# RWKV-7 state update and squared-ReLU feed-forward: the triangular inverses computed as half-chunk blocks by row substitution on GpSimd, for all heads and batches at once

## The chip, the cores and the metric

The kernel runs on one core of a Trainium2 chip. The metric is the device time of one execution in microseconds. Each core has TensorE (matrix products, with a separate weight load that overlaps them), VectorE, ScalarE, GpSimd and SyncE (SP, which only issues transfers here), each with its own instruction queue, and 16 DMA engines. In the profile they are called PE and PEld, DVE, ACT, POOL and SP.

## The reference

The input is six arrays r, k, v, w, a, b of 4 batches x 8 heads x 768 steps x 40 channels. Each batch and head carries a 40x40 state through the 768 steps; the result goes through a feed-forward block with 320 inputs, 2048 hidden units and a squared ReLU.

```python
for t in range(S):
    y[:, :, t] = np.einsum('bhd,bhde->bhe', rt, state)
    Sa = np.einsum('bhde,bhe->bhd', state, at)
    state_decay = state * wt[:, :, None, :] - np.einsum('bhd,bhe->bhde', Sa, bt)
    state = state_decay + np.einsum('bhd,bhe->bhde', vt, kt)
# x: y with heads side by side, 3072 tokens x 320
h = np.maximum(x @ w_in, 0.0)
return h * h @ w_out
```

## The kernel before

The sequence is cut into 6 rounds of 128 steps. A chunk is one round of one batch, with its 8 heads; the 24 chunks run in the order round by round, four batches in each (`order`, line 102). Within a chunk the recurrence is turned into products of 128x128 matrices for each head. The coupling between the steps of a chunk is a strictly triangular matrix N for each head, and the chunk needs the inverse of (identity + N), applied to a 128x40 block for each head. Sums of decays are kept as products from the middle of the chunk: `up` and its reciprocal `down`.

The parts of a chunk are Python generators, and a `yield` ends a step:

- `decay` (line 261): transposes of w, b and a by TensorE, cumulative products and two reciprocals by VectorE, then N from `products` (line 206), masked to the upper triangle by VectorE.
- `inverse` (line 220): the inverse by doubling of block sizes in six levels. Each level has, for the two halves of the heads, four transposes (line 235), a copy by ScalarE (line 236), four products and a masked copy (line 244), four products and an addition (line 255), each on 128x512.
- `rest` (line 282): transposes of k, r and v, the masked products A and RV, and the scaling of k and b.
- `chain` (line 314): what depends on the state of the batch: the products with A and the state, the product with the inverse (`heads(xs, g["TT"], ...)`, line 347), the new state, the masked product RX, and the output of the chunk into a `tokens` tile that holds two chunks.
- `ffn` (line 391): for every two chunks, 16 hidden tiles (48 matrix products of 256 columns), ScalarE's ReLU, VectorE's square (line 403), and the products with w_out. A step of it is used as filler, 12 for each chunk (`PER_CHUNK`).

The loop at line 438 interleaves the steps of the chain of chunk i, of `decay`, `inverse` and `rest` of chunk i+1 and of the filler. The weights come in 40 pieces, two beside each step of the inverse; they are stored as 64-bit floats, and `rounded` (line 160) turns each piece into 32-bit floats by nine VectorE instructions after a GpSimd memset (line 164, for the 24 pieces of w_in) and a transfer issued by ScalarE.

The program order is not the order in the queues. The framework plans, at build time, one fixed order for each engine from the program order and its own estimate of when each instruction is ready; on the chip each engine then takes its instructions in that order, and a transfer that must wait holds those behind it in the same queue.

## Time and profile before

| | us |
|---|---|
| median of 3 runs | 1622.65 (1622.06 to 1623.08) |
| profiled execution | 1621.3 |
| span in its profile | 1619.6 |
| TensorE busy | 1550.1 (96%) |
| VectorE busy | 971.6 (60%) |
| ScalarE busy | 315.8 (19%) |
| GpSimd busy | 24.2 (1%) |

In a row of the profile the line of the kernel comes first, then the engine, the operation, what it writes and reads, the shape and the count. Behind the first bar stand the busy time in us of the whole group and the mean duration of one instruction in ns; behind the second, how long the engine was idle just before instructions of the group, and what ended that wait. Overlapping instructions make the busy time smaller than count times mean. TensorE's fp32 products each appear as two instructions, its transposes as one.

### The profile page before, as it was taken

What the parts mean: (1) busy time and instruction counts of PE and PEld (TensorE: products, weight loads), DVE (VectorE), ACT (ScalarE), POOL (GpSimd) and SP (SyncE); (2) the same over time, 40 slices, a digit from 0 to 9 for tenths busy, and PEclk for the clock granted to TensorE, in tenths of its full rate; (3) what the DMA queues carried; (4) which work ended last, traced back from release to release, by engine and by line L of the source; (5) the groups of instructions that cost most, each with busy time, mean ns of one, the idle gap of its engine ahead of it and who ended that gap; (6) DMA issues with size and microseconds to landing.
All of it is one profiled execution on the core that took longest, in us unless ns stands there. A gap on an engine that the chain in (4) does not pass through costs nothing.

```text
span 1619.6 us, 29073 instructions
## 1 busy us (share of the span) xinstructions
PE 1550.1 (96%) x12240; PEld 1399.5 (86%) x12240; DVE 971.6 (60%) x1921; ACT 315.8 (19%) x645; POOL 24.2 (1%) x85
## 2 busy tenths in 40 slices
PE   4866899999999999999999999999999999999999
PEld 3755789899889989989989989989988988988987
DVE  5999986566555645646636636646655565564621
ACT  0111122112112112212212212212211212221211
POOL 3110000000000000000000000000000000000000
PEclk9978799999999999999999999999999999999999
DMA  8223211010100101101101001001010110000000
GB/s 96 64 61 84 67 38 18 18 27 9 22 22 14 27 17 18 27 14 22 26 11 25 13 18 31 13 18 31 9 21 19 18 22 21 15 2 9 2 6 13
DMA packets 162402, 40.87 MB, mean 25 GB/s; under 512 B 152672, under 2 KB 157664, under 8 KB 162272
## 3 DMA queue, kind: packets, MB, share of 16 engines
q1 hardware_dynamic: 156480, 28.52, 10.2%
q10 hardware_dynamic: 5792, 10.49, 2.2%
q8 instruction: 97, 1.59, 0.4%
q14 instruction: 33, 0.27, 0.1%
HBM read 34.08 MB, written 3.93 MB: 23 GB/s over the span
## 4 chain that ended last, share of the span: by engine, by line
PE 87%; DVE 6%; DMA 1%; issue 0%; ACT 0%; DVEq 0%; ACTq 0%
PE ps_w L74 35%; PE ps_f L74 27%; PE ps_c L74 12%; PE ps_w L235 7%; PE ps_w L203 4%; DMA raw<-in_moe_w_out_dram 1%; PE ps_c L353 1%; DVE inv L255 1%; PE ps_w L301 1%; PE ps_c L342 1%; DVE inv_t L227 0%; DVE N L216 0%; DVE signed L175 0%; DVE power L179 0%; DVE inv_g L244 0%; DVE inv_t L228 0%
## 5 line engine op out<-in xcount | busy, mean ns | idle before, releaser
L244 DVE TENSOR_TENSOR inv_g<-ps_w,half 128x512 f32<-128x512 f32 x288 | 197.2, 689 | 207.8 <-PE ps_w L74 205.1
L74 PE MATMUL ps_w<-inv,N 128*128 128x128 f32 x2304 | 287.4, 278 | 0.3 <-DVE RV L216 0.3
L74 PE MATMUL ps_f<-tokens,w_in 128*128 128x256 f32 x1152 | 282.2, 382 | 0.0
L74 PEld LDWEIGHTS ps_w<-inv,N 128*128 128x128 f32 x2304 | 272.7, 193 | 6.6 <-DVE RV L216 0.5
L74 PE MATMUL ps_w<-inv_g,inv_t 128*128 128x128 f32 x1920 | 239.5, 277 | 4.7 <-DVE inv_g L244 4.5
L74 PEld LDWEIGHTS ps_w<-inv_g,inv_t 128*128 128x128 f32 x1920 | 227.7, 192 | 18.0 <-issue 5.6
L255 DVE TENSOR_TENSOR inv<-ps_w,inv 128x512 f32<-128x512 f32 x240 | 165.8, 691 | 116.7 <-PE ps_w L74 115.7
L74 PEld LDWEIGHTS ps_f<-tokens,w_in 128*128 128x128 f32 x1152 | 204.7, 191 | 20.8 <-issue 0.5
L74 PE MATMUL ps_f<-w_out,hid 128*128 128x320 f32 x768 | 220.9, 433 | 0.0
L236 ACT COPY inv_t<-ps_w 128x512 f32<-128x512 f32 x240 | 130.6, 588 | 402.4 <-PE ps_w L235 374.6
L403 DVE TENSOR_TENSOR hid<-hid 128x256 f32<-128x256 f32 x192 | 80.0, 418 | 172.8 <-ACT hid L402 172.8
L74 PEld LDWEIGHTS ps_f<-w_out,hid 128*128 128x128 f32 x768 | 139.6, 190 | 47.6 <-issue 0.2
L402 ACT ACTIVATE hid<-ps_f 128x256 f32<-128x256 f32 x192 | 73.8, 385 | 331.4 <-PE ps_f L74 331.4
L235 PE MATMUL ps_w<-ident,inv 128*128 128x128 f32 x960 | 129.7, 275 | 6.3 <-DVE inv L255 6.0
L235 PEld LDWEIGHTS ps_w<-ident,inv 128*128 128x128 f32 x960 | 109.6, 141 | 26.2 <-DVE inv L255 10.2
L235 PE MATMUL ps_w<-ident,inv_t 128*128 128x128 f32 x192 | 31.9, 294 | 25.3 <-DVE inv_t L228 22.1
L255 DVE TENSOR_TENSOR inv_t<-ps_w,inv_t 128x512 f32<-128x512 f32 x48 | 33.2, 691 | 30.4 <-PE ps_w L74 29.9
L235 PEld LDWEIGHTS ps_w<-ident,inv_t 128*128 128x128 f32 x192 | 23.6, 151 | 29.9 <-issue 24.4
L74 PEld LDWEIGHTS ps_w<-inv_t,inv_g 128*128 128x128 f32 x384 | 46.4, 192 | 3.3 <-issue 0.7
L236 ACT COPY inv<-ps_w 128x512 f32<-128x512 f32 x48 | 28.1, 586 | 105.1 <-PE ps_w L235 85.6
L74 PEld LDWEIGHTS ps_w<-aT,bT 40*128 40x128 f32 x384 | 25.7, 204 | 26.1 <-DVE aT L276 19.1
L74 PE MATMUL ps_w<-aT,bT 40*128 40x128 f32 x384 | 30.6, 304 | 18.2 <-DVE aT L276 18.2
(111 smaller groups left out, 1578.9 us busy)
## 6 DMA issues: line engine op xcount, KB each, us to landing
raw<-in_moe_w_out_dram ACTq DMA_DIRECT2D x16, 320.0 KB
in_w<-in_w_dram SPq DMA_DIRECT2D x24, 160.0 KB
in_a<-in_a_dram SPq DMA_DIRECT2D x24, 160.0 KB
in_k<-in_k_dram SPq DMA_DIRECT2D x24, 160.0 KB
in_b<-in_b_dram SPq DMA_DIRECT2D x24, 160.0 KB
in_r<-in_r_dram SPq DMA_DIRECT2D x24, 160.0 KB
in_v<-in_v_dram SPq DMA_DIRECT2D x24, 160.0 KB
raw<-in_moe_w_in_dram ACTq DMA_DIRECT2D x48, 80.0 KB
```

Of the source, the lines that this page charges most:

```text
L74: nc.tensor.matmul(o, l_, r_, start=start, stop=True, skip_group_check=True)
L203: nc.tensor.transpose(p_[:, q * 128:(q + 1) * 128], pair(x_, q), ident)
L235: nc.tensor.transpose(p_[:, q], src[e][:, q], ident)
L236: nc.scalar.copy(dst[e], p_)
L244: nc.vector.tensor_tensor(gs[e], p_, over4(halves[lv]), Alu.mult)
L255: nc.vector.tensor_tensor(to, p_, to, Alu.add)
L301: nc.tensor.transpose(p_[:, q * 128:(q + 1) * 128], d_[:, q], ident)
L342: nc.tensor.transpose(p_[:, q * 128:(q + 1) * 128], st[:, q].rearrange("p e d -> p (e d)"), ident)
L353: nc.tensor.transpose(p_[:, q * 128:(q + 1) * 128], pair(xn, q), ident)
L402: nc.scalar.activation(h_, p_, Act.Relu)
L403: nc.vector.tensor_tensor(h_, h_, h_, Alu.mult)
```

## The change

N is not masked any more but copied by ScalarE and stored to DRAM for each chunk, as are `up`, `down` and the transposed and scaled a. This part is now called `early`; it runs eight chunks ahead (`LEAD`), and `rest` loads what it needs back from DRAM, one chunk ahead.

The 128x128 inverse is replaced by the inverses of its two diagonal 64x64 blocks, T, and the off-diagonal block of N is applied in the chain: the first 64 rows are solved, multiplied with the off-diagonal block, added, and then the second 64 rows are solved. The chain thus has three products of 64x64 blocks for each head in place of one of 128x128, and four more copies and products that follow one another.

The inverses of a whole round (4 batches x 8 heads x 2 blocks) are computed together by `solve`. The blocks are gathered from DRAM to `half_n`, and the 64 blocks lie on partitions, once for the even and once for the odd columns, 128 in all. Then 63 steps of two instructions each, a product and a subtraction, substitute row by row. The result goes to DRAM, and `rest` loads the part of its chunk. Round 0 is solved on VectorE while chunks 4 to 7 are prepared; round 1 on GpSimd ahead of the loop; round c+2 on GpSimd, requested behind the last chunk of round c.

The square of the hidden tile reads the product in PSUM as one of its factors. Several buffers have fewer copies. The weights are asked for in the first two passes of the loop, 20 pieces in each. The tables `first` and `halves` are gone.

```diff
-    LEVELS = 7
     GB = 2
+    LEAD = 2 * B
...
+    dram = ctx.enter_context(tc.tile_pool(name="dram", bufs=1, space=bass.MemoryType.DRAM))
...
+    def load_early(i):
+        early_loaded[i] = {nm: fetch(ring, src, i) for nm, ring, src in (("w", "w", w), ("b", "ab", b), ("a", "ab", a))}
 
     def load(i):
...
+        loaded[i] = {nm: fetch(nm, src, i) for nm, src in (("k", k), ("r", r), ("v", v), ("b", b))}
...
+    kept_n = [dram.tile([C, H, C], FP32, tag=f"n{i}", name=f"kept_n{i}") for i in range(len(order))]
...
+    kept_t = [dram.tile([B, 2, H, HC, HC], FP32, tag=f"t{c}", name=f"kept_t{c}") for c in range(NCH)]
...
+    def early(i):
...
         nc.vector.reciprocal(down[:, :, MID + 1:C + 1], up[:, :, MID + 1:C + 1])
         nc.vector.reciprocal(up[:, :, :MID], down[:, :, :MID])
+        nc.sync.dma_start(out=kept_up[i][:, :, :C + 1], in_=up[:, :, :C + 1])
+        nc.sync.dma_start(out=kept_down[i][:, :, :C + 1], in_=down[:, :, :C + 1])
...
+        nc.sync.dma_start(out=kept_a[i], in_=aT)
+        yield
+        for e, p_ in enumerate(products(bT, aT)):
+            t_ = turned("N", 2)
+            nc.scalar.copy(t_, p_)
+            nc.sync.dma_start(out=kept_n[i][:, e * NP:(e + 1) * NP, :], in_=t_)
+        yield
...
+    def solve(c, eng):
+        ns = new("half_n", [128, HC, HC], 1)
+        ts = new("half_t", [128, HC // 2, HC], 1)
+        eng.memset(ts, 0.0)
+        flat = ts.rearrange("p j t -> p (j t)")
+        for par in range(2):
+            eng.memset(flat[par * 64:(par + 1) * 64, par::HC + 2], -1.0)
+        at = 0
+        for par in range(2):
+            for bb in range(B):
+                for half in range(2):
+                    rows = slice(half * HC, (half + 1) * HC)
+                    nc.sync.dma_start(out=ns[at:at + H], in_=kept_n[c * B + bb][rows, :, rows].rearrange("s h t -> h s t"))
+                    at += H
+        yield
+        for s in range(HC - 1):
+            n, m_ = s // 2 + 1, HC - 1 - s
+            p_ = new("half_p", [128, 528], 1)[:, :n * m_].rearrange("p (j t) -> p j t", j=n)
+            eng.tensor_tensor(p_, ns[:, s, s + 1:].unsqueeze(1).to_broadcast([128, n, m_]),
+                              ts[:, :n, s:s + 1].to_broadcast([128, n, m_]), Alu.mult)
+            eng.tensor_tensor(ts[:, :n, s + 1:], ts[:, :n, s + 1:], p_, Alu.subtract)
+            yield
+        for par in range(2):
+            dst = kept_t[c].rearrange("b f h (j two) t -> (b f h) two j t", two=2)[:, par]
+            nc.sync.dma_start(out=dst, in_=ts[par * 64:(par + 1) * 64])
+        yield
...
     def rest(i, g):
...
+        nc.sync.dma_start(out=down, in_=kept_down[i][:, :, 1:C + 1])
+        nc.sync.dma_start(out=aT, in_=kept_a[i])
+        nc.sync.dma_start(out=up, in_=kept_up[i][:, :, :C])
+        with nc.allow_non_contiguous_dma(reason="two decays a head and channel"):
+            nc.sync.dma_start(out=ends[:, 0], in_=kept_down[i][:, :, 0])
+            nc.sync.dma_start(out=ends[:, 1], in_=kept_up[i][:, :, C])
...
+        g["T"], g["N"] = new("T", [128, H, HC], 2), new("N21", [HC, H, HC], 2)
+        for half in range(2):
+            nc.sync.dma_start(out=g["T"][half * HC:(half + 1) * HC], in_=kept_t[c][bb, half].rearrange("h j t -> j h t"))
+        nc.sync.dma_start(out=g["N"], in_=kept_n[i][:HC, :, HC:])
+        yield
...
     def chain(i, g):
...
-        xs = by_head(psum(ps_c))
-        heads(xs, g["TT"], lambda h: xr[:, h], True)
-        xn = minus_x.next()
-        nc.scalar.mul(xn[:, :, :D], xs, -1.0)
...
+        xr = new("xr", [128, H, D], 1)
+        nc.scalar.copy(xr[first], x_[first])
+        yield
+        xn = minus_x.next()
+        xs = by_head(psum(ps_c))
+        for h in range(H):
+            mm(xs[first, h], T[first, order_of(h)], xr[first, h], h == 0)
+        nc.scalar.copy(xn[first, :, :D], xs[first])
+        yield
+        for h in range(H):
+            mm(x_[second_, h], N[:, order_of(h)], xn[first, h, :D], False)
+        nc.scalar.copy(xr[second_], x_[second_])
+        yield
+        for h in range(H):
+            mm(xs[second_, h], T[second_, order_of(h)], xr[second_, h], h == 0)
+        nc.scalar.copy(xn[second_, :, :D], xs[second_])
...
-                nc.vector.tensor_tensor(h_, h_, h_, Alu.mult)
+                nc.vector.tensor_tensor(h_, p_, h_, Alu.mult)
...
+    run(several(range(B), prepare))
+    load(0)
+    weave((solve(0, nc.vector), HC + 1), (several(range(B, LEAD), prepare), 4 * B))
+    run(solve(1, nc.gpsimd))
+    run(rest(0, ready[0]))
     for i in range(len(order)):
+        bb, c = order[i]
+        parts = [(chain(i, ready.pop(i)), 10)]
         if i + 1 < len(order):
+            load(i + 1)
+            ready[i + 1] = {}
+            parts.append((rest(i + 1, ready[i + 1]), 6))
+        if i + LEAD < len(order):
+            parts.append((prepare(i + LEAD), 4))
+        if pieces:
+            parts.append((weights(20), 20))
+        parts.append((filler(PER_CHUNK), PER_CHUNK))
+        weave(*parts)
+        if bb == B - 1 and c + 2 < NCH:
+            run(solve(c + 2, nc.gpsimd))
```

`weave` takes its generators' steps in turn, each spread evenly over the longest of them; `several` runs a generator for each of several chunks; `prepare(i)` is the load for chunk i+1 and `early(i)`.

More of the change, by code (lines that the diff above doesn't have):

```diff
@@ L428, in run, with weave @@
             pass
-    load(1)
-    ready = {0: {}}
-    run(decay(0, ready[0]))
-    others = rest(0, ready[0])
-    for _ in inverse(ready[0]):
-        next(others, None)
-        load_weights(1)
-    run(others)
+    def weave(*gens):
+        total = max(n for _, n in gens)
+        for step in range(total):
+            for gen, n in gens:
+                for _ in range((step + 1) * n // total - step * n // total):
+                    next(gen, None)
+        for gen, _ in gens:
+            run(gen)
@@ L457 @@
-        run(this)
-        while left and i + 1 < len(order) and next(second):
-            left -= 1
+            load(i + 1)
[9 more added lines that the diff above has]
+            run(solve(c + 2, nc.gpsimd))
```

211 lines of the change are left out of this document (78 added, 133 removed).

## The prediction

> **What bounds the kernel now.** I read the page's busy lines first, then the slices of the span, then the chain of work that ended last.
>
> ```profile
> PE 1550.1 (96%) x12240; PEld 1399.5 (86%) x12240; DVE 971.6 (60%) x1921; ACT 315.8 (19%) x645; POOL 24.2 (1%) x85
> ...
> PE   4866899999999999999999999999999999999999
> ...
> PEclk9978799999999999999999999999999999999999
> ...
> PE 87%; DVE 6%; DMA 1%; issue 0%; ACT 0%; DVEq 0%; ACTq 0%
> PE ps_w L74 35%; PE ps_f L74 27%; PE ps_c L74 12%; PE ps_w L235 7%; PE ps_w L203 4%; DMA raw<-in_moe_w_out_dram 1%; PE ps_c L353 1%; DVE inv L255 1%; PE ps_w L301 1%; PE ps_c L342 1%; DVE inv_t L227 0%; DVE N L216 0%; DVE signed L175 0%; DVE power L179 0%; DVE inv_g L244 0%; DVE inv_t L228 0%
> ```
>
> TensorE is busy for all but 70 us of the span, and nearly all of that idle time lies in the first five slices. The chain of work says the same by line. Busy time by windows of 100 us (columns: length, PE, PEld, DVE, ACT, POOL with counts, granted clock, DMA share, GB/s) shows two stages with different limits:
>
> ```profile
> 0.00:100.00 100.00, 60.06 (x453) 53.65 (x455) 81.61 (x222) 11.92 (x20) 20.95 (x79) 0.92 0.47 75
> 100.00:200.00 100.00, 77.07 (x609) 68.69 (x606) 94.75 (x255) 14.56 (x28) 3.22 (x6) 0.86 0.28 75
> ...
> 300.00:400.00 100.00, 100.00 (x780) 91.31 (x779) 54.63 (x100) 19.52 (x40) 0.00 (x0) 1.00 0.08 16
> ```
>
> Up to 200 us VectorE sets the pace (94.75 us of the second 100), because it rounds the weights there beside its work for the chunks. After that TensorE has no gap. So in the main stage a change is worth what it takes from or adds to TensorE, until another engine or a queue takes its place.
>
> **What leaves TensorE.** The inverse is gone from it. Its five groups, and the one product of the chain that is replaced:
>
> ```profile
> L74 PE MATMUL ps_w<-inv,N 128*128 128x128 f32 x2304 | 287.4, 278 | 0.3 <-DVE RV L216 0.3
> L74 PE MATMUL ps_w<-inv_g,inv_t 128*128 128x128 f32 x1920 | 239.5, 277 | 4.7 <-DVE inv_g L244 4.5
> L74 PE MATMUL ps_w<-inv_t,inv_g 128*128 128x128 f32 x384 | 47.1, 276 | 0.6 <-DVE inv_g L244 0.6
> L235 PE MATMUL ps_w<-ident,inv 128*128 128x128 f32 x960 | 129.7, 275 | 6.3 <-DVE inv L255 6.0
> L235 PE MATMUL ps_w<-ident,inv_t 128*128 128x128 f32 x192 | 31.9, 294 | 25.3 <-DVE inv_t L228 22.1
> ...
> L74 PE MATMUL ps_c<-xr,inv_t 128*128 128x40 f32 x384 | 45.7, 277 | 0.5 <-DVE inv_t L255 0.5
> L74 PEld LDWEIGHTS ps_c<-RX,in_b 128*64 128x64 f32 x384 | 23.7, 144 | 2.7 <-DVE RX L216 1.5 <-issue 0.8 <-DVE power L173 0.3
> ```
>
> 287.4 + 239.5 + 47.1 + 129.7 + 31.9 = 735.6 us of busy TensorE. The product with the full inverse (16 instructions a chunk, 45.7 us in all, 119 ns each although only 40 columns stream: the 128-column weight load sets it) becomes three products of 64x64 blocks, 48 instructions a chunk. A 64-column weight load takes 23.7 / 384 = 62 ns; I take 65 ns, so 48 x 24 x 0.065 = 75 us. TensorE after: 1550 - 736 - 46 + 75 = 843 us. The feed-forward part, all transposes of inputs and all other products stay.
>
> **What leaves and enters VectorE.**
>
> ```profile
> L244 DVE TENSOR_TENSOR inv_g<-ps_w,half 128x512 f32<-128x512 f32 x288 | 197.2, 689 | 207.8 <-PE ps_w L74 205.1
> L255 DVE TENSOR_TENSOR inv<-ps_w,inv 128x512 f32<-128x512 f32 x240 | 165.8, 691 | 116.7 <-PE ps_w L74 115.7
> ...
> L227 DVE TENSOR_TENSOR inv_t<-N,first 128x512 f32<-128x512 f32 x48 | 30.9, 682 | 0.0
> ...
> L403 DVE TENSOR_TENSOR hid<-hid 128x256 f32<-128x256 f32 x192 | 80.0, 418 | 172.8 <-ACT hid L402 172.8
> L323 DVE TENSOR_TENSOR f<-f,same 128x8 f32<-128x8 f32 x20 | 3.4, 168 | 0.7
> ```
>
> About 490 of its 972 us go (197 + 166 + 31, three groups of the same size as L227, and the mask of N, which becomes a ScalarE copy). Squaring the hidden tile from PSUM instead of SBUF is nothing: L255 reads PSUM and takes 691 ns where L227 without PSUM takes 682. ScalarE gives up the inverse's copies,
>
> ```profile
> L236 ACT COPY inv_t<-ps_w 128x512 f32<-128x512 f32 x240 | 130.6, 588 | 402.4 <-PE ps_w L235 374.6
> ```
>
> and gets 48 copies of N at that 0.59 us and 48 more half-height copies in the chain; it stays under a fifth busy and the copies of N cost nothing, as N is wanted only rounds later. What enters on VectorE is the first round of the substitution. A round is 63 steps of two instructions; step s works on (s//2+1)(63-s) elements a partition, which sums to 22,352, so 44,704 elements and 126 instructions. From the rows of 512 and 256 elements: (682-418)/256 = 1.03 ns an element and about 154 ns an instruction (the 8-element row of 168 ns agrees). 44,704 x 1.03 + 126 x 0.154 = **65 us on VectorE**, once.
>
> **The other five rounds, on GpSimd.** The trace has no two-input operation there. Nearest rows:
>
> ```profile
> L164 POOL MEMSET raw<- 128x512 int32 x24 | 12.7, 533 | 101.6 <-DVE power L179 101.6
> ...
> L135 POOL MEMSET half<- 128x128 f32 x6 | 1.3, 217 | 0.0
> ...
> L121 POOL TENSOR_SCALAR_AFFINE_SELECT upper<-upper 128x128 f32<-128x128 f32 x1 | 0.3, 307 | 0.0
> ```
>
> Memsets give (533-217)/384 = 0.82 ns an element and 112 ns an instruction: the lower bound is 44,704 x 0.82 + 126 x 0.112 = 51 us a round. If two reads and the write go one after another at that rate, 2.47 ns an element, with the select's fixed 200 ns: 110 + 25 = 136 us. I take 115 us, in the upper half, since two operands must be read where the memset reads none. The Trainium skill, GPSIMD Engine Reference, section on elementwise cycle accounting, gives about 2.6 cycles an element at 1.2 GHz for this operation and advises against it there; by that estimate a round is 97 + 25 = 122 us. No run here shows it yet.
>
> Is that hidden? A round serves four chunks. TensorE needs (843 - 75 for the start - 42 for the last feed-forward group) / 22 = 33 us a chunk, 132 us for four. The substitution of round c+2 starts when N of its last chunk is written, in the fourth chunk of round c, and its result is wanted four chunks later; with some 15 us for the store of N, the 16 gathers, the store of T and its load, it needs 130 us. It fits with nothing to spare. If solves ran back to back from 170 us on, with four chunks and the last group (175 us) behind the fifth, the end would be 170 + 5(S+15) + 175 = 420 + 5S: 995 us for S = 115, below what follows. GpSimd decides from S = 143.
>
> **DMA and SyncE.** All new transfers go through SP's queue.
>
> ```profile
> q1 hardware_dynamic: 156480, 28.52, 10.2%
> q10 hardware_dynamic: 5792, 10.49, 2.2%
> ...
> 538.86 0.37 SPq L110 DMA_DIRECT2D in_v<-in_v_dram  x1
> 547.04 0.37 SPq L110 DMA_DIRECT2D in_k<-in_k_dram  x1
> ...
> 548.64 2.78 SPq L385 DMA_DIRECT2D tokens<-tokens  x4
> 551.51 0.52 SPq L110 DMA_DIRECT2D in_r<-in_r_dram  x1
> ```
>
> Small packets cost 0.102 x 16 x 1619.6 / 156480 = 17 ns of an engine, 1.8 KB ones 98 ns. After, a chunk has about 11,800 packets of 256 B and less (b is loaded twice), 2,050 of 512 B and 510 of 2 KB: some 350 engine-us, 22 us over 16 engines. SP goes from 11 issues a chunk to 29.5 (25, and 18 a round); at four in 2.8 us that is 21 us. Both fit into 33 us, at two thirds, so transfers alone add nothing; the issue order is another matter (rival below). The rows also show that this queue isn't in program order: in_v precedes in_k, which the program lists first.
>
> **The start.** Nothing of chunk 0's inverse can be used before the first four chunks are prepared, their N has gone to DRAM and back, and 126 dependent VectorE steps are done. Before, that inverse began after one chunk. The feed-forward part, 503 us of TensorE and the cover for the chain's latencies, cannot start before the weights are rounded and chunks 0 and 1 have ended. Rows for VectorE's list:
>
> ```profile
> L268 DVE TENSOR_TENSOR_SCAN decay<-ps_w,ones 128x64 f32<-128x64 f32 x96 | 25.7, 268 | 4.6 <-PE ps_w L203 4.6
> L271 DVE RECIPROCAL decay<-decay 128x256 f32<-128x256 f32 x24 | 41.4, 1725 | 0.0
> L276 DVE TENSOR_TENSOR aT<-ps_w,decay 128x512 f32<-128x512 f32 x24 | 16.3, 680 | 0.0
> L173 DVE TENSOR_SCALAR power<-power 128x256 int32<-128x256 int32 (+1 forms) x40 | 11.8, 295 | 0.0
> L179 DVE SCALAR_TENSOR_TENSOR power<-raw,signed 128x256 f32<-128x256 uint32 (+1 forms) x40 | 17.7, 443 | 0.0
> ```
>
> Each of these stands for a pair or more of its kind. A chunk's preparation: two groups each, 2 x (25.7 + 41.4 + 16.3) / 24 = 6.9 us; ten of them (eight ahead, two beside chunks 0 and 1), 69 us. Weights: 5 x 11.8 + 4 x 17.7 = 130 us. The solve, 65 us. Three chunks' products and scaling at six 0.68 us instructions each, and two chains, 17 us. Sum 281 us. In the window of 100 to 200 us VectorE ran at 0.95; 281 / 0.95 = 296, and 9 us for first loads: the feed-forward part runs freely from about **305 us**, with about 75 us of TensorE's work done (ten preparations at 3.2, three rests at 5, two chains at 11 us). The cover for all this is only TensorE's remaining early work, which is small, so the start's cost is paid nearly in full: some 230 us of idle TensorE against 70 in the whole run before.
>
> **The sum.** 843 - 75 = 768 us of TensorE remain. In the window of 300 to 400 it was at 1.00, but there the inverse's products filled the gaps between the chain's steps, and the new chain has four more hand-offs between TensorE and ScalarE. Bounds for its share: 1.00, and 0.77 as in the window of 100 to 200. I take 0.93, since the feed-forward part remains as filler and is more than half of the rest: 768 / 0.93 = 826 us. 305 + 826 = 1131 us of span, plus 1621.3 - 1619.6 = 2 us around it; the profiled execution was 1.4 us below the median of 1622.65. **Forecast 1135 us.** Its own range, by shares 1.00 to 0.85 and a start 30 us shorter or longer: 1045 to 1245.
>
> **Rivals.**
>
> *TensorE stays full and the start is shorter.* If the weights' rounding slips into the gaps between the dependent steps of the solve and loading costs less, the start is 260 us with 70 us done and the share 1.00: 260 + 773 + 2 = 1035 us. For it: rounding already interleaved with the inverse in the first windows. Against: VectorE was full there.
>
> *SP is held by the store of T.* The store waits for the last GpSimd step; every load behind it in SP's queue (k, r, v, b, decays, a, w) waits too, and behind those the next chunk's transposes. If the queue's order, fixed at build time, assumes a faster GpSimd than the chip's, a round loses up to S less one chunk of loads already in flight, 115 - 33 = 82 us; half of it, 41 us in five rounds, is 205 us: 1340 us. For it: SP's order is by expected readiness, and the row above shows such an order. Against: a store expected late stands late, and does no harm.
>
> *VectorE and GpSimd hold each other up.* During GpSimd's first round some 230 of the 360 rounding instructions are still open. If each waits for the GpSimd step in progress (0.9 us), 126 of them pass in that round, which adds about 80 us to the start: 1215 us. GpSimd's memsets of the raw weight tiles (L164, which waited 101.6 us for VectorE) stand in the same queue: where one stands among the steps, its wait for VectorE holds the steps behind it. The Trainium skill, SBUF — State Buffer, section Who interferes with whom, states such an exclusive lock for VectorE instructions with two SBUF inputs. Rows before can't show it: GpSimd only wrote.
>
> *Slower: GpSimd becomes the bound.* By 420 + 5S the end passes 1622 us from S = 240 us a round, 1.9 us a step instruction, 4.8 ns an element. At 5.5 ns an element S is 271 us and the time 1775 us. For it: the operands are broadcast along one dimension and strided by 64 elements in the other, and no row has that. Against: it is twice my upper bound.
>
> *The change doesn't do what it says* (rounds not run ahead, one chunk waiting for the next): needs solves in series with the chunks, 305 + 826 + 5 x 115 = 1706 us; the program asks for round c+2 a round early, so this needs a queue that holds everything.
>
> **Chances.** Forecast 0.50, full TensorE 0.10, lock 0.12, SP held 0.18, GpSimd the bound 0.08 (of which 0.02 ends below 1622), in series 0.02. The range 1030 to 1430 leaves out the last two and the tails of the others, some 0.17. A measurement here can tell 0.2% from no change: faster 0.91, within 0.2% 0.01, slower 0.08.
>
> **What would show it.** Right: TensorE near 840 us busy; GpSimd's step instructions of 0.9 us in mean, with idle time between rounds; VectorE full up to some 300 us and half busy after; first feed-forward products after 250 us. Wrong: SP's waits on GpSimd or on the T store of tens of us in each round (SP held); GpSimd without idle time from its first round on (the bound); VectorE rows of the rounding much longer than 295 and 443 ns while GpSimd works (lock); TensorE at 0.99 from 260 us on (full). The forecast fails above all if the start isn't set by VectorE's list or if a GpSimd step costs over 1.2 us.

## The result and the profile after

The changed kernel takes **1538.22 us** (median of 4 runs, 1534.04 to 1542.20) where the kernel before took 1622.87 us beside it (1622.06 to 1625.98): a ratio of 0.9475, 95% interval 0.9445 to 0.9505. It is faster, as predicted, but the forecast was 1135 us and its range ended at 1430 us. The profiled execution spans 1532.3 us, against a forecast span of 1131 us: 401 us are to be explained. Ratios and intervals, here and below, are taken from the faster group of executions where a kernel's executions fell into two groups, so some differ from the ratio of the medians.

The page of the changed kernel: span, busy times, the slices of TensorE, GpSimd and TensorE's granted clock, and the chain that ended last.

```profile
span 1532.3 us, 18790 instructions
...
PE 1062.4 (69%) x7248; PEld 884.2 (58%) x7248; DVE 598.7 (39%) x1330; ACT 202.1 (13%) x453; POOL 566.7 (37%) x702
...
PE   3300025009975989649989769899399994499999
...
POOL 2110000009990079920199700499500899100000
PEclk9555555556897996859967878959799887699999
...
POOL 36%; PE 32%; DMA 11%; DVE 10%; SPq 7%; issue 4%; ACTq 0%; ACT 0%; DVEq 0%; POOLq 0%
```

TensorE has three kinds of loss now. It is almost empty until about slice 9 (340 us). After that it dips at or just behind the end of each of GpSimd's five blocks of work, and its clock, 1.00 from 300 us on in before, dips too. And its busy time is 1062 us where 843 us was forecast. The chain that ended last runs through GpSimd for 36% of the span.

Three stretches of the same execution, cut at TensorE's start and at the last store of T (columns: length, then busy time of PE, PEld, DVE, ACT and POOL with counts, granted clock, DMA share, GB/s):

```profile
0.00:340.00 340.00, 57.76 (x320) 47.64 (x320) 237.65 (x620) 12.63 (x22) 21.08 (x60) 0.57 0.63 106
340.00:1310.00 970.00, 798.05 (x5540) 669.56 (x5540) 313.61 (x617) 150.63 (x340) 545.66 (x642) 0.82 0.51 80
1310.00:1532.00 222.00, 206.59 (x1388) 167.00 (x1388) 47.45 (x93) 38.85 (x91) 0.00 (x0) 0.95 0.20 42
```

GpSimd's steps themselves, by line (count, then busy us and mean ns, then its idle time ahead of them):

```profile
L268 POOL TENSOR_TENSOR half_p<-half_n,half_t 128x462 f32<-128x462 f32 (+46 forms) x315 | 255.6, 811 | 397.3 <-DMA in_k<-in_k_dram 176.1
L270 POOL TENSOR_TENSOR half_t<-half_t,half_p 128x462 f32<-128x462 f32 (+46 forms) x315 | 281.7, 894 | 24.7
```

255.6 + 281.7 = 537 us for five rounds, 107 us a round: the forecast had 115. GpSimd idles 397 us between the rounds. So it isn't slow, it is kept waiting, and what it waits for is shown by SP's waits and, further down, by SP's issues (start, length, issue; x counts issues in a row):

```profile
SPq L274 <- POOL half_t L270: 174.0, 4, 54.5
...
SPq L262 <- POOL half_p L268: 50.7, 1, 50.7
```

The first number is the wait in us, then how often, then the longest. TensorE's longest wait in total:

```profile
PE ps_w L202 <- DMA in_k<-in_k_dram: 150.9, 5, 39.5
```

And SP's issues behind two of the stores of T:

```profile
658.65 2.71 SPq L274 DMA_DIRECT2D kept_t<-half_t  x2
...
670.06 0.53 SPq L113 DMA_DIRECT2D in_k<-in_k_dram  x1
```

```profile
874.59 2.86 SPq L274 DMA_DIRECT2D kept_t<-half_t  x2
...
889.76 0.40 SPq L113 DMA_DIRECT2D in_k<-in_k_dram  x1
...
933.12 31.11 SPq L262 DMA_DIRECT2D half_n<-kept_n  x14
964.33 3.07 SPq L113 DMA_DIRECT2D in_k<-in_k_dram  x1
```

SP stands at the store of T (L274) until GpSimd's last step, 174 us in four waits. The loads of k, r, v, b for the next chunk stand behind it, so TensorE runs dry: it waits 151 us for k, in five waits. When SP goes on, it first catches up on those loads, and only then, from 933 us, comes the burst of 14 of the 16 gathers for the next round: 58 us after the store, 31 us long, 2.2 us a gather, with the loads of the next chunk behind it again. Stores follow one another by 874.59 - 658.65 = 216 us, of which GpSimd works half. Solve and chunks had become a loop through one queue.

### The profile page after: what moved, and what is told of

It reads as the page before. It is cut to its first block, busy times and chain, and to the rows that moved or that the text cites. A ratio compares the mean times of both kernels' runs of the same rounds, so it can differ in the third digit from the quotient of the medians.

```text
span 1532.3 us, 18790 instructions
## 1 busy us (share of the span) xinstructions
PE 1062.4 (69%) x7248; PEld 884.2 (58%) x7248; DVE 598.7 (39%) x1330; ACT 202.1 (13%) x453; POOL 566.7 (37%) x702
## 4 chain that ended last, share of the span: by engine, by line
POOL 36%; PE 32%; DMA 11%; DVE 10%; SPq 7%; issue 4%; ACTq 0%; ACT 0%; DVEq 0%; POOLq 0%
PE ps_f L77 19%; POOL half_t L270 19%; POOL half_p L268 17%; PE ps_c L77 8%; PE ps_w L77 2%; DMA raw<-in_moe_w_in_dram 2%; SPq L262 2%; DMA in_k<-in_k_dram 2%; DMA raw<-in_moe_w_out_dram 2%; DVE half_t L270 2%; DVE half_p L268 2%; PE ps_w L202 2%; SPq L274 1%; SPq L398 1%; DMA kept_down<-down 1%
## 5 line engine op out<-in xcount | busy, mean ns | idle before, releaser
L268 POOL TENSOR_TENSOR half_p<-half_n,half_t 128x462 f32<-128x462 f32 (+46 forms) x315 | 255.6, 811 | 397.3 <-DMA in_k<-in_k_dram 176.1
L270 POOL TENSOR_TENSOR half_t<-half_t,half_p 128x462 f32<-128x462 f32 (+46 forms) x315 | 281.7, 894 | 24.7
L416 DVE TENSOR_TENSOR hid<-ps_f,hid 128x256 f32<-128x256 f32 x192 | 81.2, 423 | 319.2 <-ACT hid L415 319.0
L77 PE MATMUL ps_c<-xr,T 64*64 64x40 f32 x768 | 65.8, 249 | 81.4 <-DMA T<-kept_t 74.5
L77 PEld LDWEIGHTS ps_c<-xr,T 64*64 64x64 f32 x768 | 59.1, 159 | 96.4 <-DMA T<-kept_t 75.0
L202 PE MATMUL ps_w<-ident,in_w 128*128 128x128 f32 x96 | 22.2, 376 | 113.9 <-DMA in_w<-in_w_dram 109.6
L229 DVE TENSOR_TENSOR_SCAN up<-ps_w,ones 128x64 f32<-128x64 f32 x96 | 26.2, 273 | 170.9 <-PE ps_w L202 169.3
L244 ACT COPY N<-ps_w 128x512 f32<-128x512 f32 x48 | 25.8, 589 | 351.0 <-PE ps_w L77 284.0
L218 DVE TENSOR_TENSOR RV<-ps_w,upper 128x512 f32<-128x512 f32 x48 | 30.9, 683 | 64.1 <-PE ps_w L77 64.1
L77 PEld LDWEIGHTS ps_c<-in_v,A 128*128 128x128 f32 x384 | 52.6, 215 | 2.4 <-ACT kvT L297 1.0
```

The source lines that it names most:

```text
L77: nc.tensor.matmul(o, l_, r_, start=start, stop=True, skip_group_check=True)
L202: nc.tensor.transpose(p_[:, q * 128:(q + 1) * 128], pair(x_, q), ident)
L218: nc.vector.tensor_tensor(t_, p_, over4(upper), Alu.mult)
L229: nc.vector.tensor_tensor_scan(up[:, q, MID + 1:C + 1], wT[:, q, MID:], ones, 1.0, Alu.mult, Alu.mult)
L244: nc.scalar.copy(t_, p_)
L268: eng.tensor_tensor(p_, ns[:, s, s + 1:].unsqueeze(1).to_broadcast([128, n, m_]), ts[:, :n, s:s + 1].to_broadcast([128, n, m_]), Alu.mult)
```

## The experiments

Line numbers in the experiments' rows are a few higher than in the changed kernel where lines were added. Kernels with all rounds on VectorE scatter by up to 2.3% between executions, so among those only larger differences, or ranges that don't overlap, are read.

### What the removal alone is worth: no_inverse

```
 before.py, inverse():
-        for lv in range(1, LEVELS): ...transposes, products, masks...
+        for _ in range(3 * (LEVELS - 1)):
+            yield
```

> The kernel before with the six levels of the inverse left out (identity plus the masked N stands for the inverse, so the states and the output are other numbers); all else stays, the full 128x128 product of the chain too. Theory A, as the prediction's first step has it (group times may be subtracted from TensorE's busy time): 1550 - 736 = 814 us of TensorE busy and a time of 885 to 930 us. Theory B (TensorE's groups overlap each other: they sum to 1723 us where the busy time is 1550, so a group is worth about 0.90 of its sum): (1723 - 736) x 0.90 = 888 us busy and a time of 960 to 1010 us.

Measured: 991.17 us (990.15 to 992.20), ratio 0.6114 (0.6102 to 0.6126).

```profile
PE 916.9 (93%) x6480; PEld 773.1 (78%) x6480; DVE 580.0 (59%) x1345; ACT 157.3 (16%) x357; POOL 24.1 (2%) x85
```

Theory B's time; its busy time of 888 us was 29 us short. TensorE's busy time falls by 1550.1 - 916.9 = 633 us and not by the 736 us to which the removed groups sum. Matmuls overlap their neighbours (277 ns each by the mean, 125 ns apart by busy time and count), and the busy time of a group counts overlap with other groups that the union counts once. The first step of the prediction took group sums out of a union: 103 us too much. The run also shows how far the idea could reach: with no substitution to wait for, and before's own order, the kernel ends at 991 us, 144 us under the forecast.

### What GpSimd's rounds cost: one_step

```
-        for s in range(HC - 1):
+        for s in range(HC - 1 if c == 0 else 1):
```

> Rounds 1 to 5 do one of the 63 substitution steps on GpSimd; 62 are left out, so T of these rounds is not the inverse. Theory A (a round is a loop of gathers, solve, store of T, and the loads of about 1.5 chunks that stand behind the store in SP's queue): SP no longer waits for GpSimd, a round takes as long as TensorE needs for four chunks, 135 to 150 us in place of 217, and the whole takes about 1105 us (1060 to 1150). Rival B (all of GpSimd's 120 us a round simply add to the rest): 1532 - 5 x 118 = 940 us.

Measured: 1368.81 us, ratio 0.8438 (0.8421 to 0.8454). Stretches of one_step, as above, cut by eye at 350 us:

```profile
0.00:350.00 350.00, 62.74 (x366) 52.74 (x367) 237.82 (x620) 13.48 (x24) 21.68 (x62) 0.56 0.64 106
350.00:1367.00 1017.00, 972.20 (x6885) 813.01 (x6883) 335.54 (x710) 188.34 (x429) 10.88 (x20) 0.92 0.53 84
```

Both theories missed. With GpSimd all but free (32.6 us of work) the kernel is 169 us faster, no more. The other 236 us of the error (1367.4 - 1131) are a start of 350 us and 972 us of TensorE work behind it, in which TensorE is 96% busy. This run splits the question in three: rounds, start, TensorE's work.

### Where GpSimd's rounds lose it: the queue

*store_late* pins the store of T of rounds 1 to 5 two chunks before the next round starts, so that SP meets it late:

```
+        if bb == B - 2 and c + 1 in stores:
+            stores.pop(c + 1)()      # the store, tc.keep_in_program_order(...)
```

> The changed kernel with the store of T of rounds 1 to 5 issued late: its place in SP's order is pinned two chunks before the first chunk that needs it, instead of wherever the planner expects GpSimd to be done. Theory A (SP, held by that store with the loads of about 1.5 chunks behind it, is what puts the rounds in series): SP's wait at the store falls from 174 us to under 40, the rounds' period from 217 us to some 160-180, and the time to 1400-1460 us. Theory B (the rounds are in series for another reason: one tile for N and gathers that queue behind loads): period and time stay, 1510-1540 us.

Measured: 1463.32 us, ratio 0.9026 (0.9009 to 0.9042). SP's waits for GpSimd in store_late:

```profile
SPq L264 <- POOL half_p L270: 119.6, 3, 50.6
...
SPq L277 <- POOL half_t L272: 64.0, 2, 47.1
```

75 us better than the changed kernel, just short of A's 1460 us: SP still stands still for 184 us, now mostly at the gathers (L264), which wait until the one tile for N is free. *late_and_behind* pins those gathers too, and moves round 1's gathers behind the loads of T of chunks 0 and 1 (the request for round 1's whole solve moves behind the loop's first pass for that):

```
+                    elif c > 1:
+                        tc.keep_in_program_order(nc.sync.dma_start(out=ns[at:at + H], ...))
```

> The store of T pinned late as in the run that did this alone (1463 us), round 1's gathers behind the loads of T as above, and the gathers of rounds 2 to 5 pinned at the end of the round that asks for them, so that SP waits for GpSimd as little as the order allows. Theory A (what is left of SP's waits for GpSimd, 120 us at the gathers and 64 at the stores, holds the loads): 1390-1430 us. Theory B (GpSimd's 125 us and the transfers around it fill a round, wherever the waits stand): 1450-1480 us.

Measured: 1458.29 us, ratio 0.8983 (0.8948 to 0.9017), Theory B's number. Its longest wait of SP for GpSimd is again the store, 231 us in five rounds. Neither place tried in SP's order suits both sides, so the next runs take both kinds of transfer off that queue. *all_gpsimd_queue* sent gathers, store and also the loads of T over GpSimd's queue:

```
-  nc.sync.dma_start(...half_n / kept_t / T...)
+  nc.gpsimd.dma_start(...half_n / kept_t / T...)
```

> All transfers that depend on the substitution (the gathers of N, the store of T and the loads of T) are issued from GpSimd's queue, so that nothing in SP's queue waits for GpSimd. All 63 steps stay. Theory A: SP's waits on GpSimd (174 us at the stores) go, loads for the next chunks run during the solve, a round takes solve 120 + gathers and transfers 30 = about 150 us, and with the start some 60 us shorter the whole takes about 1280 us (1200 to 1350). Rival B (GpSimd's time is on the path whatever the queue): 1480 to 1540 us.

Measured: 1517.24 us, ratio 0.9351 (0.9335 to 0.9367), Theory B's number. The wait only changed hands: the loads of T now wait on GpSimd's in-order queue for TensorE to free the tile T (219 us), and the steps behind them wait too. *solve_queue_gpsimd* leaves the loads of T on SP and moves only gathers and store:

```
-  nc.sync.dma_start(out=ns[...]) ; nc.sync.dma_start(out=dst, in_=ts[...])
+  nc.gpsimd.dma_start(out=ns[...]) ; nc.gpsimd.dma_start(out=dst, in_=ts[...])
```

> The changed kernel with all 16 gathers of a round and the store of T on GpSimd's own queue, where their waits for the solve cost nothing; the loads of T stay on SP. Theory A (SP's hold and the burst of gathers on SP are what made the rounds cost 170 us over the run with one step a round): 1370-1410 us. Theory B (GpSimd's rounds in series set the end, at 125 us of steps, some 15 of gathers and 10 to 20 of store and landing): a period of 150-160 us from 344 us on, the fifth round ending near 1110 us, 222 us behind it, 1340 us by that alone, so TensorE's own work would decide and the time comes out as under A; only a period over 165 us, 1430-1470 us, shows GpSimd as the bound.

Measured: 1461.04 us, ratio 0.9015 (0.9000 to 0.9030). That is in the range in which Theory B sees GpSimd as the bound, but the profile shows something else. SP no longer waits for GpSimd, and from 600 us on TensorE is busy by 95%. The loss has moved to 400 to 600 us; a window of solve_queue_gpsimd, two lines of the weights' rounding in it, and waits of GpSimd and TensorE:

```profile
400.00:500.00 100.00, 26.82 (x67) 14.99 (x65) 91.38 (x110) 3.00 (x8) 84.40 (x81) 0.50 0.14 39
```

```profile
L167 DVE TENSOR_TENSOR signed<-signed,power 128x256 int32<-128x256 int32 (+1 forms) x11 | 11.7, 1068 | 0.3
L164 DVE TENSOR_SCALAR power<-power 128x256 int32<-128x256 int32 (+1 forms) x11 | 10.3, 939 | 0.2
```

```profile
POOL raw L156 <- DVE power L171: 257.6, 13, 102.8
...
PE ps_f L77 <- DVE w_out L172: 83.8, 16, 11.4
```

The same two lines of the rounding in the changed kernel, from 60 to 300 us, where GpSimd has no steps to do:

```profile
L167 DVE TENSOR_TENSOR signed<-signed,power 128x256 int32<-128x256 int32 (+1 forms) x34 | 15.5, 456 | 1.1
...
L164 DVE TENSOR_SCALAR power<-power 128x256 int32<-128x256 int32 (+1 forms) x34 | 10.4, 305 | 0.6
```

With round 0's gathers out early the solve ran ahead of the rounding, and the rounding fell into GpSimd's first round, where the instructions shown take 2.3 to 3.1 times as long, and TensorE waits for the rounded weights (84 us for w_out's). The longest of GpSimd's waits, 102.8 us, is the memset of a raw weight tile (L156): it stands among the steps of the first round, from 307 to 410 us, waits for VectorE's rounding, and holds the steps behind it. These are both halves of the prediction's VectorE and GpSimd rival, in a place where the changed kernel, whose rounding ends before 300 us, does not meet them. *gathers_after0_gpsimd* keeps round 0 on SP, with which the rounding comes first, and moves the later rounds' gathers and stores:

```
-  nc.sync.dma_start(out=ns[...]) ; nc.sync.dma_start(out=dst, in_=ts[...])
+  (nc.sync if c == 0 else nc.gpsimd).dma_start(...)      # both
```

> The changed kernel with the gathers and the store of T of rounds 1 to 5 on GpSimd's own queue; round 0's stay on SP, so that the rounding runs ahead of the solve as in the changed kernel. Theory A (burst on SP, SP's hold, and the rounding slowed beside GpSimd are the three costs, and all three are gone): the rounding is done before 300 us, TensorE is fully loaded from 310-320 us on, 930-970 us of its work behind that: 1290-1350 us. Theory B (GpSimd's rounds set the end even when nothing stands in their way, at 160-170 us from one to the next): 1380-1450 us.

Measured: **1364.86 us** (1360.77 to 1372.13), ratio 0.8421 (0.8388 to 0.8454): between the two theories, 15 us above A's range. It is 0.887 of the changed kernel by the medians, the best that keeps the substitution, and no slower than one_step with its 62 of 63 steps left out. Its stretches, and its gathers on GpSimd's queue:

```profile
0.00:350.00 350.00, 76.92 (x514) 65.96 (x515) 244.55 (x634) 16.04 (x30) 40.78 (x92) 0.62 0.68 110
350.00:1362.00 1012.00, 946.52 (x6735) 790.68 (x6735) 356.49 (x696) 186.93 (x424) 600.80 (x701) 0.91 0.50 84
```

```profile
L262 POOL DMA_DIRECT2D half_n<-kept_n x80 | 64.3, 809 | 228.2 <-DVE half_t L270 169.0 <-DMA kept_n<-N 29.2 <-DMA half_n<-kept_n 28.9
```

GpSimd's five rounds, 107 us of steps each, cost no more here than rounds of one step do in one_step. What the transfers' places in SP's queue made of them was 1538 - 1365 = 173 us. (The edit lets the planner order everything anew, so a part of this may be a better order elsewhere; no run separates the two.)

### The start

*gather0_gpsimd* moves only round 0's gathers to GpSimd's queue:

```
-  nc.sync.dma_start(out=ns[at:at + H], ...)
+  (nc.gpsimd if c == 0 else nc.sync).dma_start(out=ns[at:at + H], ...)
```

> One edit: the 16 gathers of N for round 0 are issued from GpSimd's queue in place of SP's. In the changed kernel they go out between 74 and 183 us, and the profile puts SP's waits before them down to transfers of the raw weights. Theory A (the start is held because gathers on SP share transfer semaphores with the weights' transfers on ScalarE's queue): the gathers are out by about 90 us, the first VectorE step moves from 198 to about 100 us, and the whole is 50 to 95 us shorter, 1440 to 1490 us. Rival B (VectorE's list of 281 us sets the start): gathers early as well, but the solve only shares VectorE with the rounding and ends near 290 us as before; 1520 to 1540 us.

Measured: 1545.42 us, ratio 0.9526 (0.9495 to 0.9557), no better than the changed kernel. Gathers of round 0 in the changed kernel, then here:

```profile
107.71 75.47 SPq L262 DMA_DIRECT2D half_n<-kept_n  x11
```

```profile
73.47 7.97 POOL L262 DMA_DIRECT2D half_n<-kept_n  x10 [9.91 <-DMA kept_n<-N]
```

They leave 100 us earlier, and the solve ends near 250 us instead of 293 us, but the rounding, which had filled the wait, moves behind it and ends near 340 us. TensorE still starts only at 351 us, and it is T that it waits for, not VectorE: the loads of T stand in SP's queue behind the gathers of round 1, which take 36 us in the changed kernel and 75 us here (266.6 to 341.1 us). First the changed kernel's issue, then SP's wait in gather0_gpsimd:

```profile
298.28 36.11 SPq L262 DMA_DIRECT2D half_n<-kept_n  x15
```

```profile
SPq L262 <- DMA raw<-in_moe_w_out_dram: 61.7, 9, 14.5
```

So the wait for the transfers of the raw weights went from round 0's gathers to round 1's. The time is near Rival B's, but the run doesn't show that VectorE's list sets the start. *round1_behind* gives TensorE its first T sooner by issuing round 1's 16 gathers behind the loads of T for chunks 0 and 1 (and requesting round 1 behind the loop's first pass):

```
+  if c == 1:
+      with tc.issue_after(t_load[1].ins):
+          nc.sync.dma_start(out=ns[at:at + H], ...)
```

> The changed kernel with the 16 gathers of round 1 issued behind the loads of T for chunks 0 and 1 (before, 15 of them stand between round 0's store of T and those loads). Theory A (the late start of the feed-forward part costs its length to the end): TensorE starts about 35 us earlier, at 300-310 us instead of 335-345, and the time falls to 1495-1505 us. Theory B (the end is set by GpSimd's rounds, one after another from 344 us on, with 217 us from one to the next; an earlier start of TensorE only lengthens its later waits, and a round 1 that starts later moves all rounds): 1530-1565 us.

Measured: 1539.12 us, ratio 0.9492 (0.9478 to 0.9507). TensorE does start sooner, at 304 us in place of 344 us, and the time stays, as Theory B has it. But the burst of gathers, 35 us, now stands before chunk 2's loads, and TensorE waits 34 us for them: up to 400 us it has done 114 us of work, 110 us in the changed kernel. Whether the loop of rounds would have swallowed a real gain, as Theory B says, stays open.

### All rounds on VectorE

*all_vector* takes GpSimd out of the question:

```
-  run(solve(1, nc.gpsimd)) ... run(solve(c + 2, nc.gpsimd))
+  run(solve(1, nc.vector)) ... run(solve(c + 2, nc.vector))
```

> All rounds of the substitution run on VectorE, none on GpSimd; transfers stay on SP. A solve alone is 126 x 0.52 = 66 us there, about 85 us among VectorE's other work, against 120 us. Theory A: the loop of a round is shorter by 35 us, and the planned place of the store of T is nearer to the truth, so SP's waits at it shrink from 40 to 50 us to under 20: 1300 to 1380 us. Rival B (moving the work to VectorE, which also serves the chain, holds the chain up by as much as it saves): 1480 to 1560 us.

Measured: 1393.96 us (1371.55 to 1403.16), ratio 0.8495 (0.8447 to 0.8544), at the upper end of Theory A. VectorE at 858 us of work still has room, and a round is short there, so SP hardly stands still at the store. On this base seven variants were tried. *raw_on_gpsimd* sends the raw weights over GpSimd's queue (`nc.scalar.dma_start(out=raw...)` becomes `nc.gpsimd...`):

> All rounds of the substitution on VectorE, and the raw weights' transfers on GpSimd's queue instead of ScalarE's; to be set against the same kernel with them on ScalarE's queue (1394 us). Theory A (the gathers of round 0 leave late because each shares a completion semaphore with a raw weight transfer and waits for it): the 16 gathers are out by 110 us instead of 183, the first step of the solve runs at about 130 us instead of 198, and the time falls by 40-60 us to 1335-1355 us. Theory B (VectorE's list sets the start, and the rounding only moves behind the solve): 1380-1395 us.

Measured: 1404.43 us (1380.18 to 1408.83). Round 0's gathers are out by 100 us, so it was the raw weights that held them; but VectorE rounds first and solves until 300 us all the same. That is nearer to Theory B, and within the scatter of all_vector. *vector_store_late* adds to this the pinned store of store_late:

> The two edits above together with all rounds on VectorE: the store of T pinned late, raw weights on GpSimd's queue. Theory A (store and semaphores each hold SP): 1300-1340 us. Theory B (TensorE is 95 to 99% busy after 400 us and only the start is left): within 1% of the run with the raw weights on GpSimd's queue alone.

Measured: 1396.40 us, ratio 0.8609 (0.8592 to 0.8626). Theory B: with a quick solve the late store gains nothing. *vector_behind* adds to both round 1's gathers behind the loads of T, the same edit as in round1_behind:

> All rounds on VectorE with the late store and the raw weights on GpSimd's queue (1396 us), and round 1's gathers behind the loads of T for chunks 0 and 1. Nothing waits for GpSimd here and TensorE is 94 to 99% busy from 400 us on. Theory A (the start is a plain sum of VectorE's list, the store of T, the burst of gathers of 34 us and the loads of T): TensorE starts 34 us earlier and the time falls by as much, to 1355-1370 us. Theory B (the weights or the chain's own loads hold the start as long): 1385-1400 us.

Measured: 1428.75 us, ratio 0.8786 (0.8748 to 0.8824), slower than both theories, and its executions (1417 to 1431 us) don't overlap those of vector_store_late (1393 to 1399 us). Two windows of vector_store_late, then of vector_behind:

```profile
300.00:350.00 50.00, 1.15 (x11) 1.16 (x12) 5.67 (x18) 0.00 (x0) 0.00 (x0) 0.50 0.69 74
350.00:400.00 50.00, 47.87 (x376) 42.70 (x374) 39.93 (x81) 6.76 (x14) 0.00 (x0) 0.68 0.52 99
```

```profile
300.00:350.00 50.00, 32.30 (x252) 30.09 (x254) 11.26 (x27) 5.19 (x11) 0.00 (x0) 0.57 0.38 61
350.00:400.00 50.00, 12.10 (x79) 10.21 (x75) 15.18 (x42) 1.17 (x2) 0.00 (x0) 0.53 0.78 81
```

and SP's issues in vector_behind:

```profile
339.30 35.05 SPq L268 DMA_DIRECT2D half_n<-kept_n  x15
374.45 2.49 SPq L113 DMA_DIRECT2D in_k<-in_k_dram  x1
```

The gap moved from 300-350 to 350-400 us: behind the same 35 us burst of gathers now stand chunk 2's loads. By 400 us TensorE has done no more than without the edit, and VectorE's round 1 is later. *vector_solve_first* is vector_behind with round 0's gathers on GpSimd's queue and the raw weights back on ScalarE's:

> The run before (all rounds on VectorE, late store, round 1's gathers behind the loads of T) with the gathers of round 0 on GpSimd's queue and the raw weights back on ScalarE's: the solve of round 0 then ends near 250 us, ahead of most of the rounding, instead of near 300 us behind it. Theory A (rounding can hide behind the store and loads of T and the first chains, 40 to 60 us): 1320-1345 us. Theory B (the feed-forward part waits for VectorE's whole list either way): within 1% of the run before.

Measured: 1410.95 us (1398.66 to 1428.11), ratio 0.8675 (0.8635 to 0.8715): 1.2% below vector_behind where Theory B allowed 1%, and far from A. Here TensorE starts its chains at 261 us, but then waits 73 us for chunk 2's k, behind 72 us of round 1's gathers. *vector_gathers_gpsimd* is all_vector with every gather on GpSimd's queue, *vector_round1_gpsimd* with round 1's alone, *vector_gathers_late_store* the first of these with the store pinned:

> All rounds on VectorE (1394 us) with every gather on GpSimd's queue, which has nothing else to do. Theory A (the 34 us burst of round 1's gathers on SP stands before the loads of T and of chunk 0): TensorE starts 35 us earlier and no gap opens later, 1345-1365 us. Theory B (VectorE's whole list, rounding last, sets the start of the feed-forward part): 1385-1400 us.

> All rounds on VectorE, everything on SP's queue as in the run at 1394 us, except the 16 gathers of round 1, which go over GpSimd's queue. Theory A (that burst of 34 us before the loads of T is a plain part of the start): TensorE is loaded from 310-320 us on instead of 345-360, 1350-1370 us. Theory B (the start is set by something else, the loads for chunk 0 and the decays): 1385-1400 us.

> The run before with the store of T of rounds 1 to 5 pinned late. Theory A (the store still holds SP while VectorE ends a round): 10-30 us faster than the run before. Theory B (VectorE's rounds end long before the store is due): within 1% of it.

Measured: 1767.25 us, ratio 1.0889 (1.0844 to 1.0934); 1477.64 us, 0.9098 (0.9049 to 0.9148); 1756.04 us, 1.0843 (1.0790 to 1.0897). The first two are outside both of their theories; the third is 0.6% below the first, which fits both of its own. Transfers freed from SP made the kernel up to 373 us slower than all_vector. Waits of vector_gathers_gpsimd, and one window of it:

```profile
POOL half_n L262 <- DVE half_t L270: 760.6, 3, 281.5
PE ps_c L77 <- DMA T<-kept_t: 488.4, 5, 130.2
```

```profile
400.00:500.00 100.00, 11.96 (x62) 9.46 (x61) 91.04 (x234) 2.36 (x5) 2.62 (x5) 0.50 0.21 55
```

VectorE solves while TensorE is empty, and TensorE waits 98 us for T in each of five rounds: solves and chunks in series, the prediction's fifth rival. The steps stand later in VectorE's own order, which is fixed when the program is built: the last gather of round 2 left at 536 us and such a gather lands in some 16 us, but the round's first step came at 747 us, with VectorE 42% busy from 600 to 700 us. Why the planner put it there, no run shows.

## Why the prediction was wrong

The span of gathers_after0_gpsimd splits the 401 us, since it is the changed kernel without the loop through SP: 350 + 1012 = 1362 us where the forecast had 305 + 826 = 1131 us. The cut at 350 us is by eye.

**Rounds in series: 170 us** (1532 - 1362). The step that failed is the choice between this rival and the forecast: the rival "SP held by the store of T", at 0.18, is what happened, and its price of 205 us for five rounds was near. Its time of 1340 us was not, as it took the other two terms over from the forecast. My argument against it, that a store expected late stands late, was wrong: SP stood at the store 174 us, and TensorE waited 151 us for k. Why the planner put the store so early, no run shows. Its other half I didn't see: the gathers come as a burst, 31 us where 0.7 us an issue would make 10, and hold the loads again. The step "at two thirds, so transfers alone add nothing" was a mean over a chunk of a queue that works in bursts and in order.

**TensorE's work: 186 us** (1012 against 826). The share of 0.93 held: 946.52 / 1012 = 0.935. The 75 us done by the start came out (76.92) by luck: its own terms sum to 69 us, and the changed kernel had done 58 us by 340 us. What failed is the first step, 768 us left where 946.5 were. no_inverse shows 103 us of the difference in the subtraction of group sums; scaling them by 0.90, as its Theory B did, accounts for 74 of these. The new small products account for part of the rest:

```profile
L77 PE MATMUL ps_c<-xr,T 64*64 64x40 f32 x768 | 65.8, 249 | 81.4 <-DMA T<-kept_t 74.5
```

65.8 us for 768 of the 1152 products, 86 ns each and not 65 ns; at that, all take 99 us where 75 was forecast. What is left, some 50 us, is not in the feed-forward part, whose products sum to 495 us in gathers_after0_gpsimd and 503 us in before, but in the small products of the preparation and the chain. The slower clock is my reading of it: its mean behind 350 us is 0.91 here, against 1.00 from 300 us on in before. No run shows it.

**The start: 45 us** (350 against 305). That the solve ended at 293 us, forecast 296 + 9, is luck: VectorE had worked 238 us by 300 us, not 281, and was 0.79 busy, not 0.95; the solve's first step came only at 198 us, behind round 0's gathers, the last of which left at 183 us. What comes behind the solve was left out: the store, its landing, the loads of T and the first chain follow one after another, and none of them hides behind VectorE any more. In the changed kernel the 36 us of round 1's gathers stand among them. In gathers_after0_gpsimd these are off SP's queue and TensorE starts at 306 us, but it stands still again from 330 to 348 us, waiting for the k of a later chunk, and the start is no shorter:

```profile
300.00:350.00 50.00, 24.14 (x194) 22.18 (x195) 6.84 (x14) 3.39 (x8) 19.96 (x33) 0.57 1.06 95
```

The DMA engines are full in that window (a share of 1.06), with the same gathers among their work; that these are what delays the loads there is my reading.

**What held.** A round is 107 us of steps (115 forecast), 852 ns an instruction in mean; the 630 of five rounds never bound the kernel where they had their own queue, so neither "GpSimd the bound" nor the sum 420 + 5S of back-to-back solves decided. VectorE's busy time is 599 us where 972 - 490 + 65 = 547 was forecast, and it never was the bound behind the start. The lock of VectorE and GpSimd exists but was hardly paid, because the rounding ended before GpSimd began; only a few instructions of the chain pay it (last section). Full TensorE didn't come.

## What to carry to other kernels

Take a removed part's worth from a run without it; scaling group sums by union over sum is nearer than taking them whole (888 us against 814, measured 917). Busy times of overlapping groups don't add up. Ask of each in-order queue not how many issues it has per chunk but which instruction waits in it, for whom, and what stands behind; a transfer that depends on a slow engine goes to a queue on which nothing else is urgent. Here that engine's own was best, once the rounding's memsets were through it. Work off the critical path must be hidden in its order too: here 107 us a round cost nothing on one queue and 173 us in all on another, and a later place of the solves in VectorE's order cost 373 us.

## What the runs showed of the hardware

**VectorE beside GpSimd.** With GpSimd at two-input steps in SBUF, VectorE's rounding went from 456 to 1068 ns (two SBUF inputs) and from 305 to 939 ns (one SBUF input and a constant), which is about a GpSimd step (1040 and 1137 ns in that window, 821 and 903 ns over the run). The changed kernel pays it on the chain, in a few small instructions of each chunk; this one, a row from 300 to 470 us, takes 492 ns in one_step, where GpSimd is all but idle:

```profile
L332 DVE TENSOR_TENSOR state<-state,f 128x320 f32<-128x320 f32 x4 | 3.7, 920 | 0.1
```

The square of the hidden tile, which reads one factor from PSUM, isn't slowed there (420 ns; 424 from 461 to 537 us, between two rounds). The Trainium skill, SBUF — State Buffer, section Who interferes with whom, states an exclusive lock for two-input instructions and for tensor_scalar in its two-port modes; the rows agree with the first, and with the second if this rounding instruction ran in such a mode, which no row shows. The prediction had named the first only.

**The clock after a gap.** In windows of the changed kernel

```profile
990.00:1000.00 10.00, 7.39 (x47) 6.62 (x48) 7.49 (x13) 1.76 (x3) 9.22 (x11) 0.62 0.50 112
1000.00:1010.00 10.00, 10.00 (x60) 7.78 (x59) 4.83 (x9) 0.43 (x1) 9.29 (x10) 0.50 0.48 93
1010.00:1020.00 10.00, 9.49 (x55) 9.01 (x56) 3.77 (x10) 1.48 (x4) 9.34 (x9) 0.50 0.85 166
1020.00:1030.00 10.00, 8.98 (x57) 8.46 (x58) 3.06 (x6) 1.43 (x3) 9.33 (x9) 0.50 0.59 97
```

the granted clock falls to a half after a gap of 3.8 us (988.8 to 992.6 us) and stays there over 30 us in which TensorE is busy by 95%. After a longer gap, which ended at some 893 us, it was 0.98 from 900 to 910 us. The Trainium skill, TensorE: Matmul & The Clock Gate, section What's actually happening, gives full clock after about 3.4 us of sustained work; these rows don't agree, with busy time as the profile counts it. A gap here can thus cost more than its own length.

**Issuing.** A gather of 128 KB in 256 B pieces holds SP for 2.2 us in a burst and GpSimd for 0.81 us. The Trainium skill, DMA: Bandwidth & Descriptors, section Issuing engines are not separate DMA queues, has only the issue time to be saved by a second queue, usually little. What two queues saved here is 173 us; the wait at the store, 174 us of SP's time in the changed kernel, is no issue time at all.
